# Loads in another order, the PV and FFN work moved to match, and the last weight in seven parts: a one-token attention layer with a gated FFN on one core

## The chip, the cores and the metric

The kernel runs on one core of one Trainium2 chip. The metric is the device time of one launch in microseconds. Times given are medians over several runs; beside them stands one execution taken by the hardware profiler, whose span runs from the first to the last instruction of the program and is a little shorter than the launch. The engines are PE (TensorE, matmuls), DVE (VectorE), ACT (ScalarE), POOL (GpSimd) and SP (SyncE, which here issues the loads).

## The reference

Two tokens (batch 2, one each, 448 wide) are normalised; the result goes through an attention layer over the last 2,048 positions of a cache (16 query heads on 8 key heads of 256), and through a small FFN whose output gates it.

```python
D, Hq, Dh, Dff = 448, 16, 256, 1792            # B = 2, Hkv = 8, W = 2048 of Sk = 8192
xn = _layernorm(x)
q = (xn @ wq)                                   # per head
k, v = k_cache[:, :, Sk - W:, :], v_cache[:, :, Sk - W:, :]   # each key head serves two query heads
p = softmax(einsum("bhqd,bhkd->bhqk", q, k) * Dh ** -0.5)
s = einsum("bhqk,bhkd->bhqd", p, v).reshape(B, 1, Hq * Dh) @ wo
g = silu(relu(xn @ w1) @ w2)
return x + s * g
```

All tensors are bf16. The kernel must read 4 x 4 MB of K, as much of V, and wq, wo, w1 and w2: 44.1 MB.

## The kernel before

The work is cut into four units: unit u holds one batch and four key heads, and its K and its V are one load each of [128 partitions x 32 KB], 4 MB. K goes alternately to two buffers `kbuf`, V to two buffers `vbuf`. wq is kept in the second V buffer before V1 needs it, and wo in the first K buffer after K2 has been used. w1 and w2 have a buffer `wf` of their own.

For each unit the order of PE is: `scores(u)`, which turns K in 16 chunks (`do_T`, L294: four transposes into one of five PSUM banks `tb`, then an eviction to `kt` on DVE or ACT by the list `ON_ACT`) and multiplies it with the queries (`do_S`, in four groups); `softmax(u)`, called here the chain of unit u, which goes back and forth between DVE, PE and ACT: maximum, transposition of it, bias, shift, exponential, transposition of the weights into `pt`, sum; then `do_PV(u)`, weights times V, in four groups of 16 key slices; `attend_scale`, `attend_turn` and `attend_spread` bring its result into the layout `at_z` that the last product with wo needs. Between the steps of a chain PE has gaps, and the list given to `softmax` says what PE does in each of four of them. Before the change `gaps(u)` (L499) puts the PV of unit u-1 there, and matmuls whose result nobody reads (`idle_work`, 512 columns each): nine in chain 0 and three in each other chain. The FFN is `do_H` (first product and relu), `do_hT` (transposition) and `do_F` (second product and the gate `g_sb`).

The program writes its order out by hand: each engine executes its list in the order in which the calls stand in the source, and waits by semaphores for what the lists `deps` name. This holds for SP too, whose list is the loads: a load that waits holds back all loads that stand behind it. Issued loads go to one queue and are transferred in that order. Their waits are: `load_k(u)` for the transposes of unit u-2, `load_v(u)` for the PV of unit u-2 (V1 for the query product), the wo parts for the transposes of unit 2. The order before is wq part, K0, wq rest, K1, V0, w1, w2, K2, V1, K3, V2, V3 in two parts, wo in six parts.

The end of the kernel is the product with wo: 32 slices j of four matmuls each, accumulated in one bank; slices 0 to 15 need units 0 and 2, slices 16 to 31 units 1 and 3, and each slice needs the part of wo that holds it. `attend_spread(3)` stands inside, ahead of slice 4. Then two DVE instructions (L556, L558) and the store.

```python
            d_k[u] = pr.dma(SP, kbuf[u % 2][:, :], kv_src(u, A_k_cache), [st.get(("T", u - 2))])
            deps = [None if u == 0 else st["q_mm"] if u == 1 else st["PV", u - 2]]
            d_wo[j0] = pr.dma(SP, wo_sb[:, j0 * D:(j0 + n) * D], wo_src[v, :, j * D:(j + n) * D], [st["T", 2]])
```

Of the kernel before, what the change touches and what calls it, by code (L numbers as in the profile page):

```python
# [5 lines left out]
BF = mybir.dt.bfloat16  # L6
# [70 lines left out]
def bass_recurrent_scan__sliding_block_cached__dense_activation_relu__decode_kernel(  # L77
# [11 lines left out]
    B, Sq, D = A_x.shape  # L89
# [13 lines left out]
    SLOTS = 7  # L103
    HC = HD // 2
    FC = DFF // 2
    WO_PARTS = [8, 8, 6, 4, 4, 2]
    NWO = 16
    FIRST = 2
    NCOL = D // 4
# [1 line left out]
    GAP = NROW + 3  # L111
    NTB = 5
    ON_ACT = (1, 3, 5, 8, 10, 12, 14)
    FAR = -1.0e30
    LOW = -30000.0

    es = contextlib.ExitStack()
    with es:
        pr = _Prog(nc, es)

        def named(name, shape, dt):
            return es.enter_context(nc.sbuf_tensor(name, shape, dt))
# [4 lines left out]
        def view(t, off, dims, n=128, p0=0, pstep=1):  # L127
            width = t.shape[1]
            return bass.AP(t, p0 * width + off, [[width * pstep, n]] + dims)
# [38 lines left out]
        e_sb = named("e_sb", [128, 512], BF)  # L168
        ssum = named("ssum", [128, 1], F32)
        rs = named("rs", [128, NU], F32)  # L170
        pt = [named(f"pt{i}", [128, 512], BF) for i in range(2)]
        o_sb = named("o_sb", [128, 512], BF)
        at_exp = named("at_exp", [128, 128], BF)
        at_z = named("at_z", [128, 32 * GAP], BF)
# [43 lines left out]
        d_wq.append(pr.dma(SP, wq_sb[:, FIRST * HC:SLOTS * HC], wq_src[:, FIRST * HC:SLOTS * HC]))  # L218
        load_k(1)
        load_v(0)  # L220
        st["w1"] = pr.dma(SP, w1_sb[:, 0:W2_AT], w1_src)
        st["w2"] = pr.dma(SP, w2_sb[:, W2_AT:W2_AT + 14 * D].rearrange("p (hf f) -> p hf f", hf=2), w2_src)

        i0 = pr.op(POOL, lambda e: e.memset(ident[:, :], 0.0))
        p_id = pr.op(POOL, lambda e: e.affine_select(
# [68 lines left out]
        def do_T(u, i):  # L294
            n_th = NCHUNK * u + i
            bank, src = tb[n_th % NTB], kbuf[u % 2]
            src_f, bank_f = src[:, :].bitcast(F32), bank[:, :].bitcast(F32)
            deps = [d_k[u], p_idf, evac.get(n_th - NTB)]
            for n in range(4):
                lo = (4 * i + n) * (DH // 2)  # L300
                o = pr.op(PE, lambda e, n=n, lo=lo: e.matmul(  # L301
                    bank_f[:, n * 128:(n + 1) * 128], lhsT=src_f[:, lo:lo + 128], rhs=ident_f[:, :],
                    start=True, stop=True, is_transpose=True), deps)
                deps = []
            st["T", u] = o
            dst = kt[i]
            deps = [o, last_S.get(n_th - NCHUNK)]
            if i not in ON_ACT:
                evac[n_th] = pr.op(DVE, lambda e: e.tensor_copy(dst[:, :], bank[:, :]), deps)  # L309
            else:  # L310
                evac[n_th] = pr.op(ACTE, lambda e: e.activation(dst[:, :], bank[:, :], ACT.Copy), deps)  # L311
# [14 lines left out]
        def softmax(u, fill=()):  # L326
            fill = list(fill)

            def meanwhile():
                if fill:  # L330
                    fill.pop(0)()

            meanwhile()
            v = pr.op(DVE, lambda e: e.tensor_reduce(  # L334
                out=rm4[:, :], in_=view(sbk, 0, [[1, 4], [4, 128]]), axis=AX.X, op=ALU.max), [st["S", u]])
            v = pr.op(DVE, lambda e: e.tensor_tensor(out=rmm[:, :], in0=rm4[:, :], in1=far[:, :], op=ALU.add), [v, v_far])
            v = pr.op(DVE, lambda e: e.tensor_reduce(out=rm[:, :], in_=rmm[:, :], axis=AX.X, op=ALU.max),  # L337
                      [v, st.get(("rmT", u - 1))])
# [12 lines left out]
            v = st["shift", u] = pr.op(DVE, lambda e: e.scalar_tensor_tensor(  # L351
                out=s_sb[:, :], in0=sbk[:, :], scalar=bias[:, 0:1], in1=low[:, :], op0=ALU.add, op1=ALU.min),
                [v, v_low, st.get(("exp", u - 1))])
            meanwhile()
            a = st["exp", u] = pr.op(ACTE, lambda e: e.activation(  # L355
                e_sb[:, :], s_sb[:, :], ACT.Exp, accum_out=ssum[:, 0:1]),
                [v, st.get(("Pt", u - 1)), st.get(("gs", u - 1))])
            deps = [a, st["mbk"]]
            for j in range(4):
                o = pr.op(PE, lambda e, j=j: e.matmul(  # L360
                    mb16[:, 512 + 128 * j:640 + 128 * j], lhsT=e_sb[:, 128 * j:128 * j + 128],
                    rhs=ident[:, :], start=True, stop=True, is_transpose=True), deps)
                deps = []
            st["Pt", u] = o
            v = st["pt", u] = pr.op(DVE, lambda e: e.tensor_copy(  # L365
                view(pt[u % 2], 0, [[256, 2], [16, 16], [8, 2], [1, 8]]),
                view(mb16, 512, [[256, 2], [8, 16], [128, 2], [1, 8]])), [o, st.get(("PV", u - 2))])
            meanwhile()
            m = st["gs", u] = pr.op(PE, mm(mbk_ap(130, 1), gsum[:, :], ssum[:, 0:1], True, True), [v_gs, a, v])
            st["rs", u] = st["mbk"] = pr.op(DVE, lambda e: e.reciprocal(rs[:, u:u + 1], mbk_ap(130, 1)), [m])  # L370
            assert not fill
# [4 lines left out]
            return obk if u < NU - 1 else obk_last  # L376

        def do_PV(u, gs=range(4)):
            bank, src, p = out_bank(u), vbuf[u % 2], pt[u % 2]
            for g in gs:  # L380
                deps = [next(d for hi, d in d_v[u] if hi >= 16 * g + 16), st["pt", u], a_z if u < NU - 1 else st["tb3"], st["obk"] if u < NU - 1 else None]
                for a in range(2):
# [68 lines left out]

        def do_hT():
            hbk = tb[0][:, :].bitcast(F32).tensor
            deps = [st["h_n"], evac[2 * NCHUNK - 2]]
            for j in range(7):
                for i in range(4):
                    o = pr.op(PE, mm(view(hbk, 4 * j, [[1, 4]], n=32, p0=32 * i), view(h_n, j, [[7, 32]]),
                                     ident[:, 32 * i:32 * i + 4], j == 0, tile_position=(0, 32 * i)), deps)
                    deps = []
            st["hT"] = evac[2 * NCHUNK - 2] = pr.op(DVE, lambda e: e.tensor_copy(  # L460
                view(h_z, 3, [[GAP, 7], [7 * GAP, 2], [4, 2]]), view(hbk, 0, [[4, 7], [2, 2], [1, 2]])), [o, p_z])

        def do_F():
            fbk = tb[1][:, :].bitcast(F32).tensor
            deps = [st["w2"], st["hT"], evac[2 * NCHUNK - 1]]
            for f in range(14):
                for i in range(4):
                    lo = W2_AT + f * D + i * NCOL
# [6 lines left out]
            v_d = pr.op(DVE, lambda e: e.tensor_scalar(  # L475
                out=ea[:, :], in0=ea[:, :], scalar1=1.0, scalar2=None, op0=ALU.add), [a_e])
            v_rc = pr.op(DVE, lambda e: e.reciprocal(tmp[:, :], ea[:, :]), [v_d])
            st["g"] = evac[2 * NCHUNK - 1] = pr.op(DVE, lambda e: e.tensor_tensor(
                out=g_sb[:, :], in0=f_ap, in1=tmp[:, :], op=ALU.mult), [v_rc])

        def idle_work(n):
# [3 lines left out]
                pr.op(PE, mm(view(wbk, 0, [[1, 512]]), ident[:, :], qz[:, :], True, True), deps)  # L485
                deps = []

        def scores(u):
            for i in range(NCHUNK):
                do_T(u, i)  # L490
                if i >= 6 and i % 4 == 2:
                    do_S(u, (i - 6) // 4)
                if i == 3 and u > 1:
                    attend_turn(u - 2)
                if i == 5 and u > 1:
                    attend_spread(u - 2)
            do_S(u, 3)

        def gaps(u):  # L499
            parts = ((0,), (), (1, 2), (3,)) if u else ((), (), (), ())  # L500
            extra = (0, 1, 2, 0) if u else (2, 1, 5, 1)

            def one(gs, n):
                if gs:
                    do_PV(u - 1, gs)
                idle_work(n)
            return [lambda gs=gs, n=n: one(gs, n) for gs, n in zip(parts, extra)]

        for i in range(NCHUNK):
            do_T(0, i)  # L510
# [1 line left out]
        for g in range(4):  # L512
            do_S(0, g)
        load_k(2)
        load_v(1)
        softmax(0, gaps(0))
        scores(1)
        load_k(3)
        softmax(1, gaps(1))
        attend_scale(0)  # L520
        do_H()
        do_hT()
        do_F()
        load_v(2)
        scores(2)
        softmax(2, gaps(2))
        attend_scale(1)
        load_v(3, (0, 48, 64))
        d_wo, j0 = {}, 0
        for n in WO_PARTS:  # L530
            v, j = divmod(j0, NWO)
            d_wo[j0] = pr.dma(SP, wo_sb[:, j0 * D:(j0 + n) * D], wo_src[v, :, j * D:(j + n) * D], [st["T", 2]])
            j0 += n
        scores(3)
        st["tb3"] = pr.op(ACTE, lambda e: e.memzero(tb[3][:, :]), [evac[NU * NCHUNK - 1]])
        softmax(3, gaps(3))
        attend_scale(2)
        do_PV(3, (0, 1))
        attend_turn(2)
        do_PV(3, (2,))  # L540
        attend_spread(2)
        do_PV(3, (3,))
        attend_scale(3)
        idle_work(2)
        attend_turn(3)
# [47 lines left out]
```

## Time and profile before

| what | us |
|---|---|
| median of 7 runs | 112.5 |
| lowest and highest | 112.15, 113.02 |
| the profiled execution | 112.25 |
| its span | 110.4 |
| PE busy | 75.8 |
| DVE busy | 49.7 |
| ACT busy | 35.7 |
| DMA, mean busy share of the 16 engines by q1 | 94.1% |

Busy times are added over the span; a matmul counts from its start to its end although several are under way at once. "mean ns of one" in the groups is such a time too. A wait is put down to what released it last. The costliest groups of instructions, by line, engine and operation, with output and inputs, shapes and counts, then busy us, mean ns and the idle time just before:

```profile
L301 PE MATMUL tb<-ident_f,kbuf 128*128 128x128 f32 x256 | 34.4, 294 | 12.0 <-DMA kbuf<-in_A_k_cache_dram 12.0
L311 ACT ACTIVATE kt<-tb 128x1024 bf16<-128x1024 bf16 x28 | 27.2, 1023 | 26.9 <-PE tb L301 26.9
L309 DVE COPY kt<-tb 128x1024 bf16<-128x1024 bf16 x36 | 24.8, 691 | 22.9 <-PE tb L301 22.6
L281 PE MATMUL obk<-kbuf,at_z 128*8 128x112 bf16 x128 | 7.1, 213 | 0.8 <-DMA kbuf<-in_A_wo_dram 0.7
```

The first three are the transposes of K and their evictions, the last the product with wo. Line 281 is a helper that makes most matmuls, line 36 one that makes all loads, so these are told apart by their operands.

### The profile page before, as it was taken

The page shows a single profiled execution, that of the slowest core. Times are in us where ns is not written, and L with a number is a line of the kernel's source. Part 1 is how long each engine was busy: PE and PEld are TensorE (multiplying, and loading weights), DVE is VectorE, ACT ScalarE, POOL GpSimd, SP SyncE. Part 2 cuts the span into 40 slices and gives each one's busy share as a digit, 9 for nine tenths or more (in the row PEclk, how much of TensorE's full clock was granted, in tenths as well). Part 3 has the DMA queues.
Part 4 walks back from the last instruction along what each step waited for, and adds up shares of the span by engine and source line. Part 5 has one row for each costly group of instructions (what it writes and reads, how often), then busy time and mean ns, then how long its engine had stood idle before and what let it go on. Part 6 is the DMA issues. An engine that isn't in the chain of part 4 may idle for free.

```text
span 110.4 us, 1966 instructions
## 1 busy us (share of the span) xinstructions
PE 75.8 (69%) x862; PEld 52.6 (48%) x867; DVE 49.7 (45%) x114; ACT 35.7 (32%) x44; POOL 2.3 (2%) x12
## 2 busy tenths in 40 slices
PE   0010049995777999576674999858499967777991
PEld 0000049971225777123574977422487712325891
DVE  2292004974353855654213575554486565424001
ACT  4930005990001967020000468502096821100000
POOL 6200000000000000000000000000000000000000
PEclk9999999999999999999997699999999999999999
DMA  3999989998999999999999999999999999999930
GB/s 69 502 392 463 475 356 445 504 403 380 445 487 392 392 417 410 411 476 430 487 404 398 439 463 404 398 498 415 403 439 451 406 427 395 388 423 405 401 121 1
DMA packets 2907, 44.22 MB, mean 400 GB/s; under 512 B 338, under 2 KB 468, under 8 KB 1364
## 3 DMA queue, kind: packets, MB, share of 16 engines
q1 hardware_dynamic: 2864, 44.11, 94.1%
q8 instruction: 6, 0.10, 0.4%
q10 hardware_dynamic: 36, 0.01, 0.0%
q14 instruction: 1, 0.01, 0.0%
HBM read 44.11 MB, written 0.00 MB: 399 GB/s over the span
## 4 chain that ended last, share of the span: by engine, by line
DMA 68%; PE 22%; DVE 3%; SPq 3%; issue 1%; ACT 1%
DMA kbuf<-in_A_k_cache_dram 45%; DMA kbuf<-in_A_wo_dram 24%; PE tb L301 16%; SPq L36 3%; PE sbk L281 2%; PE obk L281 2%; PE mbk L281 1%; DVE s_sb L351 1%; ACT e_sb L355 1%; DVE rm L334 1%; DVE kt L309 1%; PE mbk L360 0%; DVE mrow L342 0%; PE mbk L339 0%; DVE tmp L556 0%
## 5 line engine op out<-in xcount | busy, mean ns | idle before, releaser
L301 PE MATMUL tb<-ident_f,kbuf 128*128 128x128 f32 x256 | 34.4, 294 | 12.0 <-DMA kbuf<-in_A_k_cache_dram 12.0
L301 PEld LDWEIGHTS tb<-ident_f,kbuf 128*128 128x128 f32 x256 | 30.9, 152 | 16.3 <-DMA kbuf<-in_A_k_cache_dram 12.3
L311 ACT ACTIVATE kt<-tb 128x1024 bf16<-128x1024 bf16 x28 | 27.2, 1023 | 26.9 <-PE tb L301 26.9
L309 DVE COPY kt<-tb 128x1024 bf16<-128x1024 bf16 x36 | 24.8, 691 | 22.9 <-PE tb L301 22.6
L281 PE MATMUL sbk<-kt,qz 128*32 128x512 bf16 x128 | 11.1, 394 | 1.6 <-DVE kt L309 1.1
L355 ACT ACTIVATE e_sb<-s_sb 128x512 bf16<-128x512 f32 x4 | 2.5, 629 | 21.4 <-DVE s_sb L351 21.4
L281 PE MATMUL obk<-kbuf,at_z 128*8 128x112 bf16 x128 | 7.1, 213 | 0.8 <-DMA kbuf<-in_A_wo_dram 0.7
L281 PE MATMUL obk<-vbuf,pt 128*16 128x512 bf16 x96 | 7.4, 380 | 0.0
L281 PEld LDWEIGHTS obk<-kbuf,at_z 128*8 128x8 bf16 x128 | 6.3, 87 | 1.4 <-DMA kbuf<-in_A_wo_dram 1.2
L281 PEld LDWEIGHTS sbk<-kt,qz 128*32 128x32 bf16 x128 | 2.7, 94 | 5.5 <-DVE kt L309 2.1
L281 PE MATMUL mbk<-ident,xg 2*128 2x2 bf16 x7 | 0.3, 163 | 6.6 <-DVE xg L246 6.6
L281 PE MATMUL tb<-qz,ident 128*128 128x512 bf16 x15 | 4.6, 382 | 0.3 <-issue 0.3
L334 DVE TENSOR_REDUCE rm<-sbk 128x4 f32<-128x512 f32 x4 | 2.8, 692 | 4.3 <-PE sbk L281 4.3
L365 DVE COPY pt<-mbk 128x512 bf16<-128x512 bf16 x4 | 1.7, 424 | 5.0 <-PE mbk L360 5.0
L281 PEld LDWEIGHTS mbk<-ident,xg 2*128 2x128 bf16 x7 | 0.3, 100 | 6.6 <-DVE xg L246 6.6
L281 PE MATMUL tb<-wf,h_z 128*8 128x112 bf16 x56 | 2.9, 213 | 0.5 <-DVE h_z L460 0.5
L351 DVE SCALAR_TENSOR_TENSOR s_sb<-sbk,bias,low 128x512 f32<-128x512 f32 x4 | 3.0, 751 | 0.1
L281 PE MATMUL mbk<-one_f,mall 1*128 1x1 f32 x8 | 1.5, 256 | 2.3 <-DVE mall L346 2.3
L339 PE MATMUL mbk<-ident_f,rm 128*1 128x128 f32 x4 | 1.1, 270 | 2.9 <-DVE rm L337 2.9
L281 PE MATMUL tb<-vbuf,pt 128*16 128x512 bf16 x32 | 2.3, 380 | 1.1 <-DMA vbuf<-in_A_v_cache_dram 1.1
L556 DVE TENSOR_TENSOR tmp<-obk,g_sb 8x112 f32<-8x112 f32 x1 | 0.3, 263 | 6.1 <-PE obk L281 6.1
L281 PEld LDWEIGHTS tb<-wf,h_z 128*8 128x8 bf16 x56 | 2.8, 87 | 0.5 <-issue 0.5
(77 smaller groups left out, 46.4 us busy)
## 6 DMA issues: line engine op xcount, KB each, us to landing
kbuf<-in_A_k_cache_dram SPq DMA_DIRECT2D x4, 4096.0 KB, 32.4
vbuf<-in_A_v_cache_dram SPq DMA_DIRECT2D x3, 4096.0 KB, 39.2
wf<-in_B_w_dram SPq DMA_DIRECT2D x2, 1568.0 KB, 43.8
vbuf<-in_A_v_cache_dram SPq DMA_DIRECT2D x1, 3072.0 KB, 18.7
vbuf<-in_A_wq_dram SPq DMA_DIRECT2D x1, 2560.0 KB, 19.5
kbuf<-in_A_wo_dram SPq DMA_DIRECT2D x2, 896.0 KB, 22.9
vbuf<-in_A_wq_dram SPq DMA_DIRECT2D x1, 1024.0 KB, 4.8
vbuf<-in_A_v_cache_dram SPq DMA_DIRECT2D x1, 1024.0 KB, 20.6
```

The lines of the kernel that those rows point to most:

```text
L36: o = _Op(eng, lambda e: e.dma_start(dst, src), [d for d in deps if d is not None], True)
L281: return lambda e: e.matmul(out_ap, lhsT=lhsT, rhs=rhs, start=start, stop=stop, skip_group_check=True, **kw)
L301: o = pr.op(PE, lambda e, n=n, lo=lo: e.matmul(bank_f[:, n * 128:(n + 1) * 128], lhsT=src_f[:, lo:lo + 128], rhs=ident_f[:, :], start=True ...
L309: evac[n_th] = pr.op(DVE, lambda e: e.tensor_copy(dst[:, :], bank[:, :]), deps)
L311: evac[n_th] = pr.op(ACTE, lambda e: e.activation(dst[:, :], bank[:, :], ACT.Copy), deps)
L334: v = pr.op(DVE, lambda e: e.tensor_reduce(out=rm4[:, :], in_=view(sbk, 0, [[1, 4], [4, 128]]), axis=AX.X, op=ALU.max), [st["S", u]])
L339: m = st["rmT", u] = pr.op(PE, lambda e: e.matmul(mbk_ap(0, 128, 1), lhsT=rm[:, :], rhs=ident_f[:, :], start=True, stop=True, is_transpose ...
L351: v = st["shift", u] = pr.op(DVE, lambda e: e.scalar_tensor_tensor(out=s_sb[:, :], in0=sbk[:, :], scalar=bias[:, 0:1], in1=low[:, :], op0= ...
L355: a = st["exp", u] = pr.op(ACTE, lambda e: e.activation(e_sb[:, :], s_sb[:, :], ACT.Exp, accum_out=ssum[:, 0:1]), [v, st.get(("Pt", u - 1) ...
L365: v = st["pt", u] = pr.op(DVE, lambda e: e.tensor_copy(view(pt[u % 2], 0, [[256, 2], [16, 16], [8, 2], [1, 8]]), view(mb16, 512, [[256, 2] ...
L556: v_t = pr.op(DVE, lambda e: e.tensor_tensor(out=tmp[:, :], in0=obk[0:NROW, 0:NCOL], in1=g_sb[:, :], op=ALU.mult), [m_o, st["g"]])
```

## The change

The loads are put into the order wq part, K0, wq rest, K1, V0, K2, K3, w1, w2, V1, V2, V3 in two parts, wo in seven parts (9, 7, 5, 4, 3, 2 and 2 slices; before 8, 8, 6, 4, 4 and 2). The PV of unit 0 stays in chain 1; the PV of unit 1 moves from chain 2 to chain 3; in its place chain 2 gets the first four chunks of transposes of unit 3, and the scores of unit 3 begin with chunk 4. The first FFN product and its transposition stand after chain 3, then the whole PV of unit 2, then the second FFN product, then the whole PV of unit 3. Of 20 idle matmuls 5 are left: three after `attend_turn(2)`, two before `attend_turn(3)`. There are three `pt` buffers, and for unit 3 another list of chunks evicted on ACT.

```diff
-    WO_PARTS = [8, 8, 6, 4, 4, 2]
+    WO_PARTS = [9, 7, 5, 4, 3, 2, 2]
...
+    ON_ACT_LAST = (0, 1, 5, 8, 10, 12, 14)
...
-        pt = [named(f"pt{i}", [128, 512], BF) for i in range(2)]
+        pt = [named(f"pt{i}", [128, 512], BF) for i in range(3)]
...
         load_k(1)
         load_v(0)
-        st["w1"] = pr.dma(SP, w1_sb[:, 0:W2_AT], w1_src)
-        st["w2"] = pr.dma(SP, w2_sb[:, W2_AT:W2_AT + 14 * D].rearrange("p (hf f) -> p hf f", hf=2), w2_src)
...
-            if i not in ON_ACT:
+            if i not in (ON_ACT_LAST if u == NU - 1 else ON_ACT):
...
-                view(mb16, 512, [[256, 2], [8, 16], [128, 2], [1, 8]])), [o, st.get(("PV", u - 2))])
+                view(mb16, 512, [[256, 2], [8, 16], [128, 2], [1, 8]])), [o, st.get(("PV", u - 3))])
...
         def do_hT():
-            deps = [st["h_n"], evac[2 * NCHUNK - 2]]
+            deps = [st["h_n"], evac[NU * NCHUNK - 4]]
...
         def do_F():
-            deps = [st["w2"], st["hT"], evac[2 * NCHUNK - 1]]
+            deps = [st["w2"], st["hT"], evac[NU * NCHUNK - 3]]
...
-        def gaps(u):
-            parts = ((0,), (), (1, 2), (3,)) if u else ((), (), (), ())
-            extra = (0, 1, 2, 0) if u else (2, 1, 5, 1)
-
-            def one(gs, n):
+        def fill(n=0, u=None, gs=(), ts=()):
+            def fn():
                 if gs:
-                    do_PV(u - 1, gs)
+                    do_PV(u, gs)
+                for t in ts:
+                    do_T(u, t)
                 idle_work(n)
-            return [lambda gs=gs, n=n: one(gs, n) for gs, n in zip(parts, extra)]
+            return fn
...
         load_k(2)
-        load_v(1)
-        softmax(0, gaps(0))
+        softmax(0)
         scores(1)
         load_k(3)
-        softmax(1, gaps(1))
+        st["w1"] = pr.dma(SP, w1_sb[:, 0:W2_AT], w1_src)
+        st["w2"] = pr.dma(SP, w2_sb[:, W2_AT:W2_AT + 14 * D].rearrange("p (hf f) -> p hf f", hf=2), w2_src)
+        load_v(1)
+        softmax(1, [fill(0, 0, (0,)), fill(), fill(0, 0, (1, 2)), fill(0, 0, (3,))])
+        load_v(2)
         attend_scale(0)
-        do_H()
-        do_hT()
-        do_F()
-        load_v(2)
-        scores(2)
-        softmax(2, gaps(2))
-        attend_scale(1)
+        scores(2, 0, {3: [lambda: attend_turn(0)], 5: [lambda: attend_spread(0)]})
+        softmax(2, [fill(0, 3, (), (0, 1)), fill(), fill(0, 3, (), (2, 3)), fill()])
+        scores(3, 4)
+        st["tb3"] = pr.op(ACTE, lambda e: e.memzero(tb[3][:, :]), [evac[NU * NCHUNK - 1]])
+        softmax(3, [fill(0, 1, (0, 1)), fill(), fill(0, 1, (2, 3)), fill()])
         load_v(3, (0, 48, 64))
...
-        scores(3)
-        st["tb3"] = pr.op(ACTE, lambda e: e.memzero(tb[3][:, :]), [evac[NU * NCHUNK - 1]])
-        softmax(3, gaps(3))
+        attend_scale(1)
+        do_H()
+        attend_turn(1)
+        do_hT()
+        attend_spread(1)
+        do_PV(2)
         attend_scale(2)
-        do_PV(3, (0, 1))
+        do_F()
         attend_turn(2)
-        do_PV(3, (2,))
+        idle_work(3)
         attend_spread(2)
-        do_PV(3, (3,))
+        do_PV(3)
         attend_scale(3)
```

The function `fill` returns what PE does in one gap: it can issue groups of a PV, transposes of single chunks, and idle matmuls. The loops over the wo slices at the end are unchanged.

More of the change, by code (lines that the diff above doesn't have):

```diff
@@ L365, in softmax @@
             v = st["pt", u] = pr.op(DVE, lambda e: e.tensor_copy(
-                view(pt[u % 2], 0, [[256, 2], [16, 16], [8, 2], [1, 8]]),
-                view(mb16, 512, [[256, 2], [8, 16], [128, 2], [1, 8]])), [o, st.get(("PV", u - 2))])
+                view(pt[u % 3], 0, [[256, 2], [16, 16], [8, 2], [1, 8]]),
+                view(mb16, 512, [[256, 2], [8, 16], [128, 2], [1, 8]])), [o, st.get(("PV", u - 3))])
             meanwhile()
@@ L378, in do_PV @@
         def do_PV(u, gs=range(4)):
-            bank, src, p = out_bank(u), vbuf[u % 2], pt[u % 2]
+            bank, src, p = out_bank(u), vbuf[u % 2], pt[u % 3]
             for g in gs:
@@ L459, in do_hT @@
                     deps = []
-            st["hT"] = evac[2 * NCHUNK - 2] = pr.op(DVE, lambda e: e.tensor_copy(
+            st["hT"] = pr.op(DVE, lambda e: e.tensor_copy(
                 view(h_z, 3, [[GAP, 7], [7 * GAP, 2], [4, 2]]), view(hbk, 0, [[4, 7], [2, 2], [1, 2]])), [o, p_z])
@@ L477, in do_F @@
             v_rc = pr.op(DVE, lambda e: e.reciprocal(tmp[:, :], ea[:, :]), [v_d])
-            st["g"] = evac[2 * NCHUNK - 1] = pr.op(DVE, lambda e: e.tensor_tensor(
+            st["g"] = pr.op(DVE, lambda e: e.tensor_tensor(
                 out=g_sb[:, :], in0=f_ap, in1=tmp[:, :], op=ALU.mult), [v_rc])
@@ L486, in idle_work, with scores @@
                 deps = []
-        def scores(u):
-            for i in range(NCHUNK):
+        def scores(u, lo=0, between=None):
+            between = between or {}
+            for i in range(lo, NCHUNK):
                 do_T(u, i)
@@ L492, in scores @@
                     do_S(u, (i - 6) // 4)
[L493 to L496, printed above, removed]
+                for fn in between.get(i, ()):
+                    fn()
             do_S(u, 3)
-        def gaps(u):
-            parts = ((0,), (), (1, 2), (3,)) if u else ((), (), (), ())
-            extra = (0, 1, 2, 0) if u else (2, 1, 5, 1)
-            def one(gs, n):
+        def fill(n=0, u=None, gs=(), ts=()):
+            def fn():
                 if gs:
-                    do_PV(u - 1, gs)
+                    do_PV(u, gs)
+                for t in ts:
+                    do_T(u, t)
                 idle_work(n)
-            return [lambda gs=gs, n=n: one(gs, n) for gs, n in zip(parts, extra)]
+            return fn
         for i in range(NCHUNK):
```

## The prediction

> **What bounds the kernel now.** I read the DMA row of the slices and the queue table first, then the end of the chain of waits, then the timelines of SP (who issues the loads) and PE, then the busy windows. The slices, the packets and the queues:
>
> ```profile
> DMA  3999989998999999999999999999999999999930
> GB/s 69 502 392 463 475 356 445 504 403 380 445 487 392 392 417 410 411 476 430 487 404 398 439 463 404 398 498 415 403 439 451 406 427 395 388 423 405 401 121 1
> DMA packets 2907, 44.22 MB, mean 400 GB/s; under 512 B 338, under 2 KB 468, under 8 KB 1364
> q1 hardware_dynamic: 2864, 44.11, 94.1%
> q8 instruction: 6, 0.10, 0.4%
> ```
>
> The reader is to see that the transfers never pause from the second slice (2.8 us) to the end of the 38th (about 105 us), and that one queue carries all 44.11 MB. 4 MB loads land 9.7 us apart (K3 at 79.0, V2 at 88.8: issue time plus time to landing), 432 GB/s. So the landing of the last byte is set by bytes, as long as SP always has the next load in the queue. The end of the chain:
>
> ```profile
> 80.63 26.18 DMA kbuf<-in_A_wo_dram
> 106.81 0.04 issue
> 106.85 1.36 PE obk L281 x24
> 108.21 0.02 issue
> 108.23 0.27 DVE tmp L556
> 108.53 0.26 DVE out_sb L558
> ```
>
> The wait ends with the fifth part of wo (80.63 + 26.18 = 106.81); 24 matmuls remain, 16 of that part and 8 of the last, which lands at 81.1 + 26.3 = 107.4 while the 16 run. What can be gained here is that tail, not the 104 us before it. PE around it, with the waits in brackets:
>
> ```profile
> 79.07 1.97 PE L301 MATMUL tb<-ident_f,kbuf 128*128 128x128 f32 x16 [1.41 <-DMA kbuf<-in_A_k_cache_dram]
> ...
> 96.09 1.04 PE L281 MATMUL tb<-vbuf,pt 128*16 128x512 bf16 x16 [0.53 <-DMA vbuf<-in_A_v_cache_dram]
> ...
> 98.58 0.61 PE L281 MATMUL tb<-vbuf,pt 128*16 128x512 bf16 x8 [0.60 <-DMA vbuf<-in_A_v_cache_dram]
> ...
> 100.05 0.26 PE L281 MATMUL mbk<-fold,o_sb 128*128 128x8 bf16 x4 [0.32 <-DVE o_sb L392]
> 100.77 0.95 PE L281 MATMUL obk<-kbuf,at_z 128*8 128x112 bf16 x16 [0.46 <-DMA kbuf<-in_A_wo_dram]
> ```
>
> PE meets each late load within about a microsecond: it has little slack at the end, but it waits for DMA, not DMA for it. SP's issues:
>
> ```profile
> 24.08 0.55 SPq L36 DMA_DIRECT2D kbuf<-in_A_k_cache_dram  x1
> 25.71 0.54 SPq L36 DMA_DIRECT2D vbuf<-in_A_v_cache_dram  x1
> 44.16 0.53 SPq L36 DMA_DIRECT2D kbuf<-in_A_k_cache_dram  x1
> 50.77 27.75 SPq L36 DMA_DIRECT2D vbuf<-in_A_v_cache_dram  x3
> ```
>
> K3 is issued at 44.16 and lands 34.9 us later, behind everything ahead of it: the queue is deep. Last, the clock: in the windows below the columns PE, PEld, DVE, ACT, POOL are busy us, then the granted clock.
>
> ```profile
> 56.09:59.51 3.42, 1.24 (x26) 1.07 (x22) 1.31 (x3) 0.25 (x1) 0.00 (x0) 1.00 1.02 436
> 59.51:62.92 3.41, 3.38 (x16) 3.38 (x17) 1.21 (x2) 1.02 (x1) 0.00 (x0) 0.50 1.04 442
> 97.05:100.46 3.41, 2.17 (x30) 0.76 (x27) 1.39 (x4) 0.00 (x0) 0.00 (x0) 1.00 1.03 422
> ```
>
> A window with PE busy for 1.24 of 3.42 us (0.36) is followed by one at clock 0.50; one with 2.17 of 3.41 (0.64) is not.
>
> **What the Trainium skill says.** "DMA: Bandwidth & Descriptors", Issuing engines are not separate DMA queues and Where 436 GB/s comes from: all loads share the same 16 engines, with a ceiling of 435 GB/s. The trace agrees, with 432 GB/s over a 4 MB load. "Runtime: NRT & Kernel Launch", Instruction fetch mechanics: instructions come in 16 KiB blocks by DMA. The trace has six such packets on q8, and K1 lands 11.15 us after the load before it instead of 9.7, with one of them between. "TensorE: Matmul & The Clock Gate", What's actually happening: after an idle window of about 3.4 us PE runs at half clock until it has been busy for one. The trace agrees on half clock and length (3.41 us), but shows that PE 36% busy already counts as idle, so I take the threshold as between 0.36 and 0.59 (the lowest share that kept the clock, 76.57 to 79.99: 2.01 of 3.42).
>
> **The change part by part.** (1) The order of the loads, at 0. No byte is added. From 42.2 us, when V0 has landed, the landings become (9.7 us each for 4 MB, 3.8 for w1 and w2, which landed 3.8 apart before): K2 51.9, K3 61.6, w1 65.4, w2 69.2, V1 79.0, V2 88.7; then V3 and wo at the old times. SP's waits decide whether the queue stays full. K3 still waits for the transposes of unit 1 (44.2), and w1, w2 and V1, now queued behind it on SP, follow within 3 us; 51.9 is 5 us away at the least. V2 waits for the PV of unit 0 (51 us), with 28 us to spare. V3 waits for the PV of unit 1, now in chain 3, and the seven wo loads stand behind it on SP. That PV needs V1 (79.0) and the end of the scores of unit 3. These I add up: scores of unit 2 from 51.9 take 11.0 us warm (79.07 to 90.03 in the trace) or 12.6 us cold (59.54 to 72.13), end 62.9 to 64.5; chain 2 about 5.8 us (5.5 from last score to row sum in the trace, 0.3 taken for the transposes of unit 3 put inside), end 68.7 to 70.3; the other 12 chunks 9.0 us, end 77.7 to 79.3. So chain 3 runs from about 79 to 85, and the second half of PV of unit 1 ends at about 83. The queue would be dry at 88.7, less some 2 us from issue to flow (the first load, issued at 0.73, moves little before 2.0): 3.7 us are left.
>
> (2) Work moved from before the gap to after: the FFN's first half (0.84 + 0.54 us on PE, 0.39 and 0.25 on DVE between) runs from 86 to 88.2, before V2 lands. PV of unit 2 (four times 0.54) 88.7 to 90.9, F 2.9 us to 93.8, turn 0.26, three idle matmuls 0.65; its g chain on DVE (0.25 on ACT, 0.21 + 0.84 + 0.26, 1.7 with gaps) ends at 95.5, and the turn's product is queued behind it there (0.29), the spread and so PV of unit 3 behind that on PE: 96.1. V3's first part lands at 96.05. Cost 0, with no more than 0.1 us of cover there; but if this slips by a microsecond, only the wait for V3's second part at 98.53 shrinks, since three quarters of that PV are 1.6 us. If all is 1.5 us late, wo starts late by about 0.7 and the end by 0.4.
>
> (3) Idle matmuls: 20 before, 5 after. They are hidden in the softmax chains; PE saves nothing that the end sees. What they covered is the clock. Without them the window after the scores of unit 0 has 0.6 + 0.27 + 0.38 = 1.25 us of work, about 0.37, near the share that went cold. A cold window costs the transposes behind it 3.60 - 1.97 = 1.6 us, which (1) has room for. From both sides: 0 to 1.6 us on PE, 0 at the end; I take 0.
>
> (4) The third pt buffer and the other evictions on ACT: one wait less, and one DVE copy (0.69 us) of four taken out of the DVE chain of unit 2. Both lie before 70 us, under the loads: 0.
>
> (5) wo in seven parts. One j of wo is 114,688 B, 0.274 us of DMA in large parts (98.53 to 100.72 for eight) and 0.28 in small ones; on PE it is four matmuls, 49 ns from start to start, 0.197 us. Parts of 9, 7, 5, 4, 3, 2, 2 land at 101.0, 102.9, 104.3, 105.4, 106.25, 106.8, 107.4. PE: nine from 101.03 with the last spread between (0.21) to 103.0; seven to 104.4; five to 105.4; four from 105.45 to 106.25; three from 106.3 to 106.9; two to 107.3; the last two from 107.4. So 8 matmuls stand after the last landing instead of 24 after 106.85: the last one starts at 107.41 + 7 x 0.049 = 107.75 instead of 106.85 + 23 x 0.049 = 107.98. Gain 0.23 us. The extra part adds eight packets to each DMA engine; a packet of 1,792 B took about 4 ns more than its bytes at 27 GB/s, and one of 7,168 about 9, so 0.03 to 0.07 us; I take 0.05.
>
> Sum: -0.23 + 0.05 = -0.2 us. The profiled execution took 112.25 us (span 110.4, 1.8 around it), so it would take 112.05. The median of the seven runs is 112.5, 0.25 above the profiled one; I carry that along: 112.3.
>
> **The rivals.** (A) As summed, 112.3. (B) Faster by more, about 111.9: the 0.25 us between profile and median is PE late at the end, because K3 lands at 79.0 and 16 us of scores and softmax must fit before V3 at 96.05. The wait of 1.41 us before 79.07 sits where a window in another phase would go cold; 1.6 us more on the scores pushes the chain's end from 95.2 past 96.05. The change brings K3 forward by 17 us and would take this away. Against it: PE catches most of this up in wo (0.197 against 0.274 us per j). (C) Slower, 113.4: the clock falls in the wo matmuls. From the end of three quarters of the last PV (97.6) to the first wo matmul (101.0), PE is busy for 0.61 + 0.6 + 0.26 = 1.5 us of 3.4, 0.43, where before it also had a turn, a spread and a PV quarter, and 0.59. If a window falls there and 0.43 is under the threshold, matmuls take 98 ns from 101.0 for up to 3.4 us: 7 j are done by 104.4 instead of 14 or more, PE is then the bound, and the 25 left end about 1.1 us later. It decides if the window starts within about 97.3 to 97.9, a sixth of its phases. (D) Nothing gained, or something lost, at the DMA: an instruction packet falls on an engine that is already late, and as all 16 must land the end moves by up to the 1.4 us that K1 lost; 112.6 to 113.7. (E) The queue runs dry: if V3 is issued after about 86.7, each microsecond is a microsecond at the end; at 88 it is 113.6. Two cold windows before it would do this. That the change doesn't do what it says I exclude for the order of PE's instructions; whether the removed idle matmuls were needed is C and E.
>
> **How the numbers follow.** A 0.53, B 0.24, C 0.11, D 0.07, E 0.05. A measurement of this kernel tells 0.3%, about 0.34 us, from no change. A lies at -0.2 us with some 0.2 either way: 0.15 faster, 0.36 same, 0.02 slower. B: 0.22 faster, 0.02 same. C: 0.10 slower, 0.01 same. D: 0.05 slower, 0.02 same. E: 0.05 slower. Faster 0.37, same 0.41, slower 0.22. The range runs from B with 0.2 us more, 111.7, to 113.1, which takes in A, most of D and the near parts of C and E, and leaves out about 0.15. A's own range is 112.1 to 112.5.
>
> **What would show it.** The last wo part lands at 107.3 to 107.5, and the chain ends with 8 wo matmuls after it, not 24; the last starts 0.2 us earlier. The DMA row has no digit below 8 between the first and the last slices; V3 is issued at 82 to 84. PV of unit 3 starts within 0.5 us of 96.05. Clock 0.50 may show before 90 us at no cost; after 100 us it is C. A landing of the last part beyond 107.8 is D or E, told apart by a gap in the DMA row. A landing before 107.0 would mean that the order of loads itself saves transfer time, which I have excluded.

## The result and the profile after

The changed kernel takes 113.65 us (median of 27 runs, 112.08 to 115.02) against 112.44 for the kernel before (64 runs, 112.15 to 113.81); the forecast was 112.3, with a range to 113.1. The ratio is 1.0051 with a 95% interval of 1.0028 to 1.0074; it leaves out runs more than 1.5% above the fastest, two in five of the changed kernel's, and so lies under the ratio of the medians, 1.011. The spread tells more than the middle: some runs are as fast as forecast, and most are 1 to 2.5 us slower.

The profiled execution took 113.62 us, span 111.8. Two rows of its slices, the granted clock and the DMA share in tenths:

```profile
PEclk9999999999975599999999999589999557999999
DMA  3989989989989988998998999999989999999810
```

The DMA row has no digit below 8 between its first and last slices, as forecast, and q1's mean share is 93.2%, before 94.1%; the clock has three dips where it had one. The end of the chain of waits (start, length, what):

```profile
86.41 20.57 DMA kbuf<-in_A_wo_dram
107.02 1.99 PE obk L280 x36
109.02 0.57 PE obk L280 x8
109.62 0.27 DVE tmp L557
109.91 0.26 DVE out_sb L559
```

Only 8 matmuls stand after the last landing, as forecast, but it comes at 109.0 instead of 107.4. The last wait of PE is an earlier one: it ends at 106.98 (86.41 + 20.57), with the fourth part of wo, forecast for 105.4, and the 44 matmuls behind it run without a gap. So the transfers ended 1.6 us later. Was PE late? Its timeline at the end (start, length, what; in brackets the idle time before and what ended it):

```profile
98.46 1.90 PE L280 MATMUL tb<-vbuf,pt 128*16 128x512 bf16 x32
...
102.10 0.95 PE L280 MATMUL obk<-kbuf,at_z 128*8 128x112 bf16 x16 [0.62 <-DMA kbuf<-in_A_wo_dram]
...
107.02 2.56 PE L280 MATMUL obk<-kbuf,at_z 128*8 128x112 bf16 x44 [0.42 <-DMA kbuf<-in_A_wo_dram]
```

PV of unit 3 starts 2.4 us later than the forecast's 96.05, and still the wo product begins by waiting for its first part. In this execution DMA was late, not PE.

Where was the time lost, if the DMA row is full? Each load has 16 landings in the trace, one for each DMA engine, and it is there with the last of them; the row is a mean over the engines. The packets of the trace can be counted: how many are under way at each moment. Before the change, 16 at every moment from 6 to 104 us. After it (one engine without work for 1 us is 1 engine-us):

```
49.9 to 50.9 us   15
86.4 to 88.4 us   14 or 15
engine-us without work: 1.1 and 2.2
```

These are the moments at which K2 and V2 end, the loads ahead of K3 and V3. I call such an engine dry: K3 and V3 were issued too late for it. SP's issues of the changed kernel near K3:

```profile
46.52 0.54 SPq L36 DMA_DIRECT2D kbuf<-in_A_k_cache_dram  x1
```

and near V3:

```profile
83.61 1.18 SPq L36 DMA_DIRECT2D vbuf<-in_A_v_cache_dram  x2
```

K3 went out 2.4 us later than before (44.16), since the transposes of unit 1 before it began 0.5 us later and took longer. PE's timeline, before the change:

```profile
34.81 3.25 PE L301 MATMUL tb<-ident_f,kbuf 128*128 128x128 f32 x28
```

and after it:

```profile
35.28 5.14 PE L300 MATMUL tb<-ident_f,kbuf 128*128 128x128 f32 x28
```

The same 28 transposes, 5.14 us instead of 3.25. The windows of the changed kernel say why (PE, PEld, DVE, ACT, POOL busy us, then the granted clock, the DMA share, GB/s):

```profile
28.92:32.33 3.41, 1.19 (x15) 0.39 (x7) 1.84 (x7) 0.00 (x0) 0.00 (x0) 1.00 1.05 452
32.33:39.16 6.83, 4.93 (x25) 4.67 (x26) 2.54 (x5) 1.93 (x4) 0.00 (x0) 0.50 1.07 461
```

Before the change, the window at this place had 2.19 us of PE work (0.64), and the clock stayed up:

```profile
28.79:32.20 3.41, 2.19 (x19) 0.80 (x13) 1.77 (x7) 0.00 (x0) 0.00 (x0) 1.00 1.08 461
```

With 1.19 of 3.41 us (0.35; step 3 of the prediction had said 0.37) the clock is halved for two windows.

A dry engine alone is 1.1 us behind, which the landings absorb, since the last engine is 1.4 us behind the others anyway: the instruction blocks (16 KB each, six in this run) come over the same engines and cost the one they use some 1.45 us (1.0 for the block itself, 0.5 on the packet after it). It hurts when the two add up. The 16 landings of K3 and of w1 behind it in the changed kernel's trace, us:

```
K3  59.8 59.8 59.8 59.9 59.9 59.9 59.9 60.0 60.0 60.1 60.1 60.2 60.9 61.2 61.5 61.5
w1  63.5 63.6 63.6 63.6 63.6 63.7 63.7 63.7 63.7 63.9 63.9 64.0 64.6 65.2 65.3 66.5
```

A common step is 3.75 us. The two 61.5 become 65.2 and 65.3; the 61.2 becomes 66.5, and an instruction block went out at 61.32. The trace does not name the engines, but on a busy engine a packet starts within some nanoseconds of the end of the one before, so an engine can be followed. The one that was dry from 49.82 to 50.98 ended its first packet of w1 at 61.322, the only packet that ended there, and the block started at 61.319: the dry engine took the block. It was not the first to finish K2, so the first engine is a measure of the queue and not the one that must run dry.

This engine is then the last to land each load up to the third part of wo (105.4, the next one 104.3), and lands the last part at 108.5. The 109.0 belongs to another engine: it took the block of 104.72 inside the fourth part and landed that part at 107.0, the one for which PE waited. At the third part five engines were 1.8 to 2.0 us behind the first, and it was one of them; whether from an earlier block or from V3's late issue the small packets of wo don't tell. So K3's late issue accounts for about 1.1 of the 1.6 us here, and the rest is a block on an engine that was already late.

### The profile page after: what moved, and what is told of

Its sections match the earlier page's. It is cut to its first block, busy times and chain, and to the rows that moved or that the text cites. A ratio compares the mean times of both kernels' runs of the same rounds, so it can differ in the third digit from the quotient of the medians.

```text
span 111.8 us, 1942 instructions
## 1 busy us (share of the span) xinstructions
PE 77.1 (69%) x851; PEld 54.4 (49%) x852; DVE 49.2 (44%) x114; ACT 35.9 (32%) x44; POOL 2.3 (2%) x12
## 3 DMA queue, kind: packets, MB, share of 16 engines
q1 hardware_dynamic: 3008, 44.11, 93.2%
## 4 chain that ended last, share of the span: by engine, by line
PE 48%; DMA 31%; DVE 12%; SPq 3%; ACT 2%; issue 2%
PE tb L300 29%; DMA kbuf<-in_A_wo_dram 18%; DMA kbuf<-in_A_k_cache_dram 13%; PE sbk L280 8%; PE obk L280 5%; PE mbk L280 3%; SPq L36 3%; DVE rm L333 3%; DVE s_sb L350 2%; ACT e_sb L354 2%; DVE kt L308 2%; PE mbk L359 1%; DVE mrow L341 1%; PE mbk L338 1%; DVE mall L345 1%
## 5 line engine op out<-in xcount | busy, mean ns | idle before, releaser
L300 PE MATMUL tb<-ident_f,kbuf 128*128 128x128 f32 x256 | 36.0, 301 | 8.4 <-DMA kbuf<-in_A_k_cache_dram 8.4
L300 PEld LDWEIGHTS tb<-ident_f,kbuf 128*128 128x128 f32 x256 | 32.5, 158 | 13.3 <-DMA kbuf<-in_A_k_cache_dram 8.5
L280 PE MATMUL obk<-vbuf,pt 128*16 128x512 bf16 x96 | 8.1, 463 | 0.7 <-DMA vbuf<-in_A_v_cache_dram 0.7
L359 PE MATMUL mbk<-ident,e_sb 128*128 128x128 bf16 x16 | 1.8, 243 | 4.2 <-ACT e_sb L354 4.2
L280 PEld LDWEIGHTS obk<-vbuf,pt 128*16 128x16 bf16 x96 | 2.3, 100 | 4.1 <-issue 1.7
L391 DVE TENSOR_SCALAR o_sb<-obk,rs 128x512 bf16<-128x512 f32 x3 | 2.2, 738 | 4.1 <-PE obk L280 4.1
L359 PEld LDWEIGHTS mbk<-ident,e_sb 128*128 128x128 bf16 x16 | 1.0, 105 | 5.5 <-ACT e_sb L354 5.5
```

The source lines that it names most:

```text
L280: return lambda e: e.matmul(out_ap, lhsT=lhsT, rhs=rhs, start=start, stop=stop, skip_group_check=True, **kw)
L300: o = pr.op(PE, lambda e, n=n, lo=lo: e.matmul(bank_f[:, n * 128:(n + 1) * 128], lhsT=src_f[:, lo:lo + 128], rhs=ident_f[:, :], start=True ...
L359: o = pr.op(PE, lambda e, j=j: e.matmul(mb16[:, 512 + 128 * j:640 + 128 * j], lhsT=e_sb[:, 128 * j:128 * j + 128], rhs=ident[:, :], start= ...
L391: v = st["osb", u] = pr.op(DVE, lambda e: e.tensor_scalar(out=o_sb[:, :], in0=view(out_bank(u), 0, [[1, 512]]), scalar1=rs[:, u:u + 1], sc ...
```

## The experiments

All times are medians, beside runs of the kernel before on the same chip; a ratio has its 95% interval in brackets. I had two theories: P, the half clock from the missing idle matmuls, and Q, the order, which puts V3 and wo on SP behind a PV that needs V1. Two more, L and S, come with the fifth experiment. Only one execution of each kernel is traced, and the moments of issue differ between executions: with the same code ahead of it, K3 went out at 46.52, 46.90, 47.76 and 47.85 us in four of the traces below.

**Idle matmuls back in all chains**

```diff
-        softmax(0)
+        softmax(0, [fill(2), fill(1), fill(5), fill(1)])
...
-        softmax(1, [fill(0, 0, (0,)), fill(), fill(0, 0, (1, 2)), fill(0, 0, (3,))])
+        softmax(1, [fill(0, 0, (0,)), fill(1), fill(2, 0, (1, 2)), fill(0, 0, (3,))])
...
-        softmax(2, [fill(0, 3, (), (0, 1)), fill(), fill(0, 3, (), (2, 3)), fill()])
+        softmax(2, [fill(0, 3, (), (0, 1)), fill(1), fill(2, 3, (), (2, 3)), fill()])
...
-        softmax(3, [fill(0, 1, (0, 1)), fill(), fill(0, 1, (2, 3)), fill()])
+        softmax(3, [fill(0, 1, (0, 1)), fill(1), fill(2, 1, (2, 3)), fill()])
```

> The changed kernel with idle matmuls put back into all four chains (9 in chain 0, 3 in each other one). Theory P (the half clock): the mean clock rises from 0.92 to 0.97 or more, K3 is issued at about 44.5 us instead of 46.5, PV of unit 3 starts within 0.5 us of V3's landing, and the time falls to 112.0 to 112.5, a ratio to before of 1.00 or less. Theory Q (the order: V3 and wo stand on SP behind a PV that needs V1): the time stays at 113.2 or more, ratio above 1.004, with V3 still issued after 83 us and single DMA engines without work at 86 to 88 us.

Measured: 112.22, ratio 0.9976 (0.9953 to 0.9999), clock 0.969 in the profile. SP and PE of its trace:

```profile
44.47 0.53 SPq L36 DMA_DIRECT2D kbuf<-in_A_k_cache_dram  x1
```

```profile
35.12 3.25 PE L300 MATMUL tb<-ident_f,kbuf 128*128 128x128 f32 x28
```

The transposes are fast again, K3 goes out 2 us earlier, no engine is dry. The loss is gone: P, but by which way is open. PV of unit 3 starts at 98.05 even here, 2 us after V3's first part, at no cost; that part of the expectation was wrong. The wo product still starts at 101.09, right behind the landing of its first part at 101.05.

**Idle matmuls in chain 0 alone** (the first edit of these four)

> The changed kernel with the nine idle matmuls of chain 0 alone put back. Theory P, early part (K3 issued late because the transposes of unit 1 run at half clock): K3 is issued at about 44.3 us, no DMA engine is without work at 50 us, the last landing moves from 109.0 back to about 107.5, and at least half of the loss goes: 112.5 to 113.0. If only the late part counts (clock after 84 us, or V3's issue), the time stays within 0.3 us of the changed kernel's median, 113.3 to 113.9.

Measured: 113.22, ratio 0.9992 (0.9949 to 1.0034), runs from 112.04 to 114.73. In its profile K3 is issued at 44.74 with no dry engine there, but V3 only at 84.95, since half clocks lie at 50 to 57 and 71 to 74 us, and engines are dry for 3.85 engine-us. The time lies between the two expectations. In the profiled execution, one of the slower ones (113.94), K3 was mended and V3 was late instead.

**PV of unit 1 wholly in the first gap of chain 3**

```diff
-        softmax(3, [fill(0, 1, (0, 1)), fill(), fill(0, 1, (2, 3)), fill()])
+        softmax(3, [fill(0, 1, (0, 1, 2, 3)), fill(), fill(), fill()])
```

> The changed kernel with all four groups of the PV of unit 1 in the first gap of chain 3, so that V3 is issued about 2 us earlier (81.5 instead of 83.6 us) and chain 3 ends about 1 us later. Theory Q: no engine without work at 86 to 88 us, and the time falls by 0.5 us or more, to 113.1 or less. Theory P: no gain, 113.4 to 114.2, since PE is later at the end by up to 1 us.

Measured: 113.41, ratio 1.0034 (1.0005 to 1.0064). V3 was issued at 83.03 with nothing dry behind it, but K3 at 47.76, with 4.6 engine-us dry. Q in this form falls, though the edit moved V3 by 0.6 us only, as K3 and V1 came later.

**The kernel before with wo in seven parts**

```diff
-    WO_PARTS = [8, 8, 6, 4, 4, 2]
+    WO_PARTS = [9, 7, 5, 4, 3, 2, 2]
```

> The kernel before with wo in seven parts and nothing else. Both theories and the prediction's step 5: 8 instead of 24 matmuls after the last wait, 0.2 us less than before: ratio 0.997 to 1.000. If the seventh part's packets cost more than taken, 1.000 to 1.002.

Measured: 112.19, ratio 0.9971 (0.9949 to 0.9993); the kernel before beside it 112.46. The step of the sum that was to bring 0.2 us brought 0.27, and the new order with idle matmuls (112.22) brings nothing beyond it. Three of the 22 runs lie above 113, and the profiled execution is one of them, 113.73. In it the clock is 0.50 from 101.35 to 104.76, inside the wo product:

```profile
97.94:101.35 3.41, 1.86 (x23) 0.48 (x15) 1.41 (x4) 0.00 (x0) 0.00 (x0) 1.00 0.99 407
101.35:104.76 3.41, 3.28 (x35) 3.07 (x36) 0.23 (x1) 0.00 (x0) 0.00 (x0) 0.50 1.01 400
```

The first 16 wo matmuls take 1.66 us instead of 0.95, and PE runs from there to the end without a wait. That is rival C of the prediction, here in the old order.

**The order of before, seven parts, no idle matmuls in the chains**

```diff
-            extra = (0, 1, 2, 0) if u else (2, 1, 5, 1)
+            extra = (0, 0, 0, 0)
```

> The kernel before with wo in seven parts, and the 18 idle matmuls of its four chains taken out; order of loads and of PE's work as before. It tells whether the lost idle matmuls cost by PE being late at the end (theory L) or by loads issued too late for a short queue (theory S). S: the queue of this order is deep (V3 issued before 80 us for an end of V2 at 87 to 89), so no DMA engine is without work and the time is that of the run with seven parts, 112.2, ratio 0.996 to 1.000. L: as slow as the changed kernel, 113.2 to 113.9.

Measured: 114.52. The ratio, 1.001 (0.9955 to 1.0065), rests on five of the 14 runs and shows no difference; the other nine lie at 113.87 or more. The profiled execution, 114.5, is one of the nine, and it fits theory L. No engine is dry in its trace and the last part lands at 107.6, but the end of its chain is PE alone:

```profile
103.86 0.88 PE obk L281 x16
104.85 5.62 PE obk L281 x112
110.49 0.27 DVE tmp L556
```

The wo product starts at 103.8, 2.6 us after its first part has landed, and never waits. By the medians, though not by the ratios, the missing idle matmuls cost more in the old order, where K3 lands at 79 and PE has little slack, than in the new one.

**Idle matmuls in chains 2 and 3 alone** (the last two edits of the first experiment)

> The changed kernel with idle matmuls in chains 2 and 3 alone (three each), none in chains 0 and 1: the early half clock stays, so K3 is still issued at about 46.5 us. If K3's late issue is a cause of its own, 112.8 to 113.4 and an engine without work near 50 us; if only the late part counts, 112.1 to 112.5.

Measured: 113.48, ratio 1.0019 (0.9981 to 1.0057); K3 at 47.85, and 1.5 engine-us dry near 50 us. The idle matmuls of the late chains are not enough.

**More in the queue, no idle matmul**: half of w2 ahead of K3, and five slices of wo ahead of V3

```diff
         load_k(2)
+        load_w2(0)
         softmax(0)
...
-        st["w2"] = pr.dma(SP, w2_sb[:, W2_AT:W2_AT + 14 * D].rearrange("p (hf f) -> p hf f", hf=2), w2_src)
+        load_w2(1)
...
-    WO_PARTS = [9, 7, 5, 4, 3, 2, 2]
+    WO_PARTS = [5, 4, 7, 5, 4, 3, 2, 2]
...
-        load_v(3, (0, 48, 64))
         for n in WO_PARTS:
+            if j0 == 5:
+                load_v(3, (0, 48, 64))
...
-        do_PV(3)
+        do_PV(3, (0, 1, 2))
```

The last group of that PV and its turn then stand behind the fifth slice of wo, its spread behind the ninth; `load_w2` issues one half of w2.

> The changed kernel, no idle matmul put back, but with more in the queue ahead of the two loads that were issued late: half of w2 ahead of K3, and the first five slices of wo ahead of V3 (their matmuls ahead of the last PV group). Theory S: the mean clock stays near 0.92, no engine is without work at 50 or at 86 to 88 us, and the time falls to 112.2 to 112.7. Theory L: the holes go, the time stays above 113.2.

Measured: 112.26, ratio 0.997 (0.9943 to 0.9996), with a mean clock of 0.92 in most runs, as low as the changed kernel's. Theory S holds for the median in the new order: the half clock costs through late issues. It is not all: six of the 22 runs lie above 113, and the profiled execution is one of them, 114.09. No engine is dry in it and the last part lands at 107.8, but PV of unit 3 starts at 100.4, and the end of the chain is PE alone, as in the old order without idle matmuls:

```profile
104.39 0.88 PE obk L280 x16
...
105.39 4.63 PE obk L280 x92
```

So a late PE remains as a second way, in the slowest runs. Then each edit alone.

Half of w2 ahead of K3:

> The changed kernel with half of w2 ahead of K3 and nothing else (the first of the two edits of the deeper queue). No engine without work near 50 us, those near 86 to 88 us remain. If each late load has a cost of its own: 112.7 to 113.3. If K3's alone decides: 112.2 to 112.5; if V3's alone: 113.4 to 113.9.

Measured: 112.22, ratio 0.9962 (0.9935 to 0.9989).

Five slices of wo ahead of V3:

> The changed kernel with the first five slices of wo ahead of V3 and nothing else (the second of the two edits). An engine without work near 50 us remains, none at 86 to 88 us. If each late load has a cost of its own: 112.7 to 113.3. If V3's alone decides: 112.2 to 112.5; if K3's alone: 113.4 to 113.9.

Measured: 113.27, ratio 1.0023 (0.9992 to 1.0054), 4.5 engine-us dry near 50 us and none behind V3. A late K3 alone is enough for most of the loss. The run with half of w2 shows what removes it; its SP and its PE:

```profile
25.18 0.60 SPq L36 DMA_DIRECT2D wf<-in_B_w_dram  x1
47.08 0.54 SPq L36 DMA_DIRECT2D kbuf<-in_A_k_cache_dram  x1
```

```profile
35.73 5.24 PE L300 MATMUL tb<-ident_f,kbuf 128*128 128x128 f32 x28
```

The transposes are as slow and K3 as late as in the changed kernel, and the loss is gone, as 0.8 MB more were queued ahead of it. The dry engines expected near 86 to 88 us did not come: V3 went out at 82.62 there, a microsecond earlier than in the changed kernel. So this run does not tell what V3's own lateness costs.

**Late issues with the clock unhurt**: idle matmuls in all chains, and one more wait ahead of K3 (for the transposed maximum of chain 1; its load and the three behind it stand after that chain in the source) or ahead of V3 (for the exponential, then for the last step, of chain 3). The wait of K3:

```diff
-            d_k[u] = pr.dma(SP, kbuf[u % 2][:, :], kv_src(u, A_k_cache), [st.get(("T", u - 2))])
+            d_k[u] = pr.dma(SP, kbuf[u % 2][:, :], kv_src(u, A_k_cache), [st.get(("T", u - 2)), st["rmT", 1] if u == 3 else None])
```

> The changed kernel with idle matmuls in all four chains, and K3 (with w1, w2 and V1 behind it on SP) made to wait for the transposed maximum of chain 1, so that it is issued at about 46.9 us instead of 44.5 while the clock stays at 0.95 or more. Theory S at K3: engines without work at 50 us, last landing past 107.8, median 112.9 to 113.8 against 112.2 without the wait. If the half clock itself is the cost: 112.1 to 112.4.

Measured: 112.96, ratio 1.0007 (0.9978 to 1.0036), runs from 112.16 to 116.19, clock 0.954. K3 was issued at 46.83; the profiled execution had no dry engine near 50 us all the same, and took 0.7 us more than the first experiment's. The median is 0.7 us higher too, but the intervals of the two ratios overlap: that a late K3 costs without a half clock before it is likely and not shown, and this one profile doesn't show how it would.

> The changed kernel with idle matmuls in all four chains, and V3 made to wait also for the exponential of chain 3, so that it is issued at about 84 us instead of 82.4 with the clock unhurt (mean 0.95 or more). Theory S (issue too late for a short queue): engines without work at 86 to 88 us, and a median of 112.7 or more against 112.2 without the wait. If only the clock matters, 112.1 to 112.4.

Measured: 112.21, ratio 0.9945 (0.9919 to 0.9971). V3 went out at 83.37, not 84, and only 0.1 engine-us were dry: too weak a test.

> The changed kernel with idle matmuls in all four chains, and V3 made to wait for the last step of chain 3, so that it is issued at about 85 us, with some 1.8 us left until the first engine has finished V2. If a late V3 costs like a late K3: engines without work at 86 to 88 us and a median of 112.9 or more. If V3's issue does not matter: 112.1 to 112.4.

Measured: 113.77, ratio 1.0057 (1.0023 to 1.0091), clock 0.969 in the profile, 4.5 engine-us dry at 86 to 89 us. V3's issue in that trace:

```profile
84.69 1.18 SPq L36 DMA_DIRECT2D vbuf<-in_A_v_cache_dram  x2
```

A V3 later than that of the changed kernel by 1.1 us costs 1.5 us beside the first experiment, with the mean clock unhurt; here the intervals lie apart.

**K2 cut into four loads**, so that smaller packets lie ahead of K3

> The changed kernel, no idle matmul put back, with the load of K2 cut into four by columns, so that the packets that lie in the queue ahead of K3 are 8 KB instead of 32 KB; K3 is issued as late as in the changed kernel. If the time that a load has to be issued ahead is that of a number of packets in the queue, no engine is without work near 50 us and the median is 112.2 to 112.6. If it is a fixed time of some 4 us, the engines without work stay and the median is 113.2 or more.

Measured: 112.8, ratio 1.0014 (0.999 to 1.0038); 0.3 engine-us dry near 50 us in the profile, with K3 as late as 47.6. Ten of the 22 runs were under 112.65. With 2.6 us of lead that is little beside 4.6 in the run with PV of unit 1 first (2.3 us), but the time lies between the two expectations: not settled.

**Versions to keep.** Five more idle matmuls at the tail of the kernel before with seven parts:

> The kernel before with wo in seven parts and five more idle matmuls between the first wait for V3 and the wo product. If the clock in the wo product is what makes the rare slow executions of the kernel with seven parts alone (one in seven above 113.2), they go and the median is 112.1 to 112.2, ratio 0.996 to 0.998; if not, nothing changes: 112.2 with as many above 113.

Measured: 112.23, ratio 0.9955 (0.9929 to 0.9981), three of 22 runs above 113 as without them: nothing gained.

The deeper queue and the idle matmuls together:

> The deeper queue and the idle matmuls in all four chains together, on the order of the change: as good as either alone, 112.1 to 112.3, ratio 0.996 to 0.998, with fewer executions above 113. A ratio below 0.995 would mean that something else than these two still costs time.

Measured: 112.23, ratio 0.9958 (0.9939 to 0.9977), and none of 22 runs above 113, where the kernel before beside it had 26 of 74. It beats both kernels, and is the steadiest.

## Why the prediction was wrong

- **The tail, step (5).** Right in size where the seven parts stand alone: 0.27 us gained (0.23 - 0.05 forecast). In the changed kernel's profile 8 matmuls stand after the last landing, but PE's last wait is one for the fourth part.
- **No byte added, step (1).** Right: in most traces of seven parts without dry engines the last part lands at 107.45 to 107.9 (forecast 107.4); in the run with K3 late it was 108.1.
- **PE before the last PV, step (2).** Wrong, at little cost: PV of unit 3 starts 2.0 us late even in the first experiment, since the clock is 0.50 from 87 to 94 us there and PV of unit 2 takes 3.59 instead of 2.2 us.
- **The idle matmuls, step (3).** Taken at 0, and wrong. "A cold window costs the transposes behind it 3.60 - 1.97 = 1.6 us, which (1) has room for" was right in its first half: the cold transposes cost 1.9 us and K3 went out 2.4 us later. The room was not there.
- **The room in step (1).** This is the step that failed, by a mis-sized term. "51.9 is 5 us away at the least" takes the landing of K2, that of its slowest engine; the first engine is done with K2 at 50.0 (its own update of the semaphore). And "some 2 us from issue to flow" is too short. Issue time, the moment at which the first engine has finished the load ahead, and the engine-us without work:

```
run                 load  issued  first done  lead  dry
changed             K3    46.52   50.03       3.5   1.1
changed             V3    83.61   86.78       3.2   2.2
PV1 first           K3    47.76   50.04       2.3   4.6
idle in chain 0     V3    84.95   86.76       1.8   3.9
idle in 2 and 3     K3    47.85   50.14       2.3   1.5
idle in 2 and 3     V3    83.41   86.90       3.5   0.3
wo5 ahead of V3     K3    46.90   50.11       3.2   4.5
V3 later            V3    84.69   86.86       2.2   4.5
K3 late             K3    46.83   50.23       3.4   0
V3 late             V3    83.37   86.77       3.4   0.1
PV1 first           V3    83.03   87.17       4.1   0
w2 half ahead       V3    82.62   86.90       4.3   0
w2 half ahead       K3    47.08   52.10       5.0   0
idle in all chains  K3    44.47   50.12       5.7   0
```

  With 1.8 to 3.5 us of lead engines ran dry in nine of ten cases, with 4.1 or more in none. (Where half of w2 goes ahead, it is the load ahead of K3; in all other rows that is a 4 MB load.) I had counted 51.9 - 44.2 = 7.7 us for K3, and 5 for the loads behind it, with some 2 needed. From 46.52 to the first engine it was 3.5, and that was too little. V3's issue at 83.61 lies inside the forecast of 82 to 84, with 3.7 us said to be left, and engines were dry all the same.
- **The rivals.** E, the queue that runs dry, was the mechanism, given 0.05 and put at V3 with its threshold at 86.7. K3's late issue is enough for most of the loss (113.27 with V3 in time); what V3's costs at 83.61 was not separated, and its point lies near 83.4. D, an instruction packet on an engine that is late already, is how it reaches the end; I had taken the two for alternatives, and they add. C, a half clock in the wo product, is not in the profile of the changed kernel, whose clock is full from 93.8 us on; it is in the slow execution of the kernel before with seven parts.
- **The test I named.** "A gap in the DMA row" could not tell: one dry engine of 16 for a microsecond is some 2% of a slice of 2.8 us.
- **Open:** whether the slowest runs of the changed kernel (above 114) also have PE late. The traced executions of the deeper queue (114.09) and of the old order without idle matmuls (114.5) did, with no engine dry; the changed kernel has only the one trace, of 113.62.

## What to carry to other kernels

In a kernel bound by one queue of loads, what counts is not when a load is needed but when it is issued against the first engine to run out of the load ahead: count that lead for each load that waits, from the first engine to finish and not from the landing. Work that looks useless on an engine that isn't the bound, here matmuls that nobody reads, may be what keeps an issue on time. A small load without a wait, put ahead of one that waits, bought the same time here at no measured cost.

## What the runs showed of the hardware

PE's clock was halved after a window with PE busy for 0.35, and in the kernel before after 0.36; 0.59 kept it there. A threshold of the busy share between these, as the prediction took it, does not hold everywhere: in the changed kernel's own trace a window with 0.62 was followed by a half clock,

```profile
66.47:69.88 3.41, 2.12 (x19) 1.70 (x19) 2.61 (x6) 1.04 (x3) 0.00 (x0) 1.00 1.20 510
69.88:73.29 3.41, 3.41 (x21) 2.24 (x20) 1.47 (x3) 1.02 (x1) 0.00 (x0) 0.50 0.98 423
```

and in the first run with V3 late one with 0.44 (76.85 to 80.26 us) kept it. What else counts is open.

Behind 32 KB packets loads with up to 3.5 us of lead mostly left engines dry. One with 2.2 us behind a part of wo left none, whose packets are 4.5 KB (the deeper queue's V3, issued at 85.95 with the first engine done at 88.2). This looks as if a number of packets ahead mattered rather than a time, but the run with K2 cut into four did not settle it.
